# Banded attention and rational MLP in one kernel: scores and values in 64x32 tiles of TensorE, and a fixed issue order for the first three row tiles

## The chip, the cores and the metric

The kernel runs on one core of a Trainium2 chip. The time is device time in microseconds of one execution; three runs of the kernel before are given, and one further execution was recorded by the hardware profiler.

## The reference, cut to what matters

Eight batches of 576 positions, eight heads of 64 columns. Each query sees the 128 keys up to and including itself, with a bias that falls linearly with distance. The result, 4608 rows of 512 columns, goes through an MLP of width 2048 whose activation is a ratio of two polynomials.

```python
scores = scale * np.matmul(q, k.transpose(0, 1, 3, 2))
bias = slopes[:, None, None] * (-np.abs(rel).astype(np.float32))[None, :, :]
mask = (rel >= 0) & (rel < window)              # window = 128, rel = query - key
scores = np.where(mask, scores + bias[None], -1000000000.0)
attn = np.exp(scores - max); attn = attn / (sum + 1e-09)
x = np.matmul(attn, v)                           # heads side by side: 4608 x 512
h = x @ w_in; h2 = h * h; h3 = h2 * h            # 512 x 2048
P = a[0] + a[1] * h + a[2] * h2 + a[3] * h3
Q = 1.0 + np.abs(b[0]) * np.abs(h) + np.abs(b[1]) * h2
out = (P / (Q + 1e-06)) @ w_out                  # 2048 x 512
```

## The kernel before, in words

**Tiles.** The 4608 rows are 36 blocks of 128 rows, in 18 row tiles of two blocks. Heads go in pairs (four pairs `p`), one head of a pair on partitions 0 to 63 and the other on 64 to 127. The attention of one pair over one or two blocks is a **unit** (`attention(u)`, L411). Row tile 0 has eight units of one block, every other row tile four units of two blocks. Every ninth block (`kind == 1`, `own_only`) begins a batch and sees only its own keys.

**A unit.** TensorE makes the scores (`scores`, L441, matmuls at L456, result in PSUM tiles `sc0` and `sc1`, one per head). VectorE folds them into a dense 128x128 form: `copy_predicated` (L490) takes, where a mask says so, a score from a neighbouring column group, and L497 adds the bias and finds the row maximum. ScalarE takes the exponential (L502), VectorE the reciprocal of the sums (L510, L511), GpSimd scales the rows (`pr`, L512). TensorE transposes `pr` (L523); ScalarE copies the result into `p_all` (L529, L530, L532), GpSimd splits it into the part that belongs to the block's own keys and the part that belongs to the block before (L536). TensorE then multiplies with the values (`quarters`, L597, matmuls at L607, into PSUM tiles `px` and `py`; for row tile 0 and the last units of its kind `values`, L568, matmul L575), and ScalarE and VectorE bring the sum of both to SBUF as `x`, split into a coarse and a fine part (`x_hi`, `x_lo`).

**Tiles of TensorE.** Scores contract over the 64 columns of a head, so the array is used as 64 rows by 64 columns four times over (`tile_position=(64 * h, Q * half)`, `Q` = 64): the row half holds the head, the column half holds 64 of the 128 queries. The first 64 queries of a block need two calls (128 keys strided over the block before, then 64 own keys), the second 64 one call of 192 keys:

```python
elif half:
    todo = [(slice(0, 3 * Q), own - Q, own + P)]
else:
    todo = [(slice(0, 3 * Q, 2), own - P, own), (slice(Q, 2 * Q), own, own + Q)]
```

`quarters` uses the same four tiles: there the row half holds 64 keys and the column half one head's 64 value columns. From row tile 2 on, one plan entry issues the transposes of one unit, the scores of the next and the values of an earlier one back to back. This piece of TensorE's order is called a session here.

**MLP.** For each row tile and each of 16 chunks of 128 hidden columns, `up` (L730) makes `h` and `down` (L793) adds into `acc`; three fp32r matmuls for each product (`hi*hi`, `lo*hi`, `hi*lo`). In the first passes over row tiles 0 to 2 a chunk whose weights aren't split yet is used as plain fp32 (`is_plain`). The activation between them is L757 to L775 on ScalarE, GpSimd and VectorE.

**Weights.** They come as 64-bit numbers in 32 halves of 512 KB, one `raw_w` per chunk and matrix (loads L661 and L663), and `convert` turns each into fp32 with one step on GpSimd (L666), one on ScalarE (L667) and two on VectorE (L668, L669). `split` (L672) later makes the coarse and fine parts (L683, L684).

**Order.** Every step is an entry of `Plan` with costs per engine and a due time. `Plan.order` (L116) plays the entries through on modelled engines and queues, always the ready entry that is due first, and the order that comes out is the order in which the program issues them. All loads stand in SP's queue. The due times come from some sixty constants (L273 to L279).

## Time and profile before

| | us |
|---|---|
| three runs | 1016.33, 1017.22, 1017.29 (median 1017.22) |
| the profiled execution | 1016.81 |
| its span, first to last instruction | 1015.1 |
| TensorE (PE) busy | 997.9, 98% of the span |
| VectorE (DVE) busy | 789.5, 78% |
| ScalarE (ACT) busy | 693.0, 68% |
| GpSimd (POOL) busy | 513.7, 51% |

PE is the matmul stream, PEld the loading of stationary operands, which runs beside it. A plain fp32 matmul leaves two records in the trace, an fp32r one leaves one. A matmul's record holds its way through the array too, so records overlap, and the rate of a stream is read from the distance of the starts, not from the length of a record. `PEclk` is the granted share of TensorE's full clock.

### The profile page before, as it was taken

How to read it: one execution, taken by the hardware profiler on the slowest of the kernel's cores; microseconds unless marked ns; L12 is line 12 of the kernel's file. 1: busy time of each engine (PE TensorE's matmuls, PEld its weight loads, DVE VectorE, ACT ScalarE, POOL GpSimd, SP SyncE). 2: the span in 40 equal slices, each digit the busy share in tenths (PEclk: the TensorE clock that was granted, in tenths of full speed). 3: DMA queues.
4: the chain of work that ended last, by engine and by line, in shares of the span. 5: the costliest groups of instructions: out<-in, count | busy, mean ns of one | idle time of the engine just before them, and what ended most of it. 6: DMA issues, size and time to landing. Idle time of an engine off the chain costs nothing.

```text
span 1015.1 us, 24014 instructions
## 1 busy us (share of the span) xinstructions
PE 997.9 (98%) x9095; PEld 866.7 (85%) x9095; DVE 789.5 (78%) x1942; ACT 693.0 (68%) x1729; POOL 513.7 (51%) x567
## 2 busy tenths in 40 slices
PE   8899998999999999999999999999999999999998
PEld 4667777988888989998989999898898898998897
DVE  4889979788786878777787768787887786878775
ACT  5769777677766767676776666676766676767553
POOL 3757868454544544454555445544544544534432
PEclk7899999999999999999999999999999999999999
DMA  8845202111111111121211112021111211200000
GB/s 286 298 167 177 81 31 74 35 56 57 52 55 56 62 51 67 43 67 44 70 43 44 52 47 70 30 80 34 61 61 46 65 64 35 79 17 22 1 23 21
DMA packets 45139, 69.05 MB, mean 68 GB/s; under 512 B 4448, under 2 KB 29664, under 8 KB 45024
## 3 DMA queue, kind: packets, MB, share of 16 engines
q1 hardware_dynamic: 44736, 67.26, 20.5%
q8 instruction: 71, 1.16, 0.5%
q14 instruction: 44, 0.36, 0.1%
q10 hardware_dynamic: 288, 0.26, 0.1%
HBM read 58.07 MB, written 9.44 MB: 67 GB/s over the span
## 4 chain that ended last, share of the span: by engine, by line
PE 89%; POOL 3%; DMA 2%; DVE 2%; ACT 2%; issue 1%; SPq 0%; ACTq 0%; DVEq 0%; POOLq 0%
PE h L730 39%; PE acc L793 38%; PE sc L456 5%; PE px L607 4%; DMA raw_w<-in_w_in 1%; PE sc L523 1%; PE px L523 1%; POOL w_lo L684 1%; POOL g_q L760 1%; PE py L607 1%; POOL g_q L758 1%; DMA kq<-in_kqv 0%; POOL raw_w L666 0%; PE px L575 0%; DMA id_sb<-in_ident 0%
## 5 line engine op out<-in xcount | busy, mean ns | idle before, releaser
L730 PE MATMUL h<-x_hi,wi_hi 128*128 128x256 f32 x1024 | 289.2, 282 | 0.3 <-ACT x L612 0.2
L730 PE MATMUL h<-x_lo,wi_hi 128*128 128x256 f32 x1024 | 288.1, 281 | 0.2 <-DVE x_lo L618 0.2
L730 PE MATMUL h<-x_hi,w_lo 128*128 128x256 f32 x1024 | 287.5, 281 | 0.0
L758 POOL TENSOR_SCALAR g_q<-g_u,babs 128x512 f32<-128x512 f32 x144 | 112.1, 778 | 221.5 <-ACT g_u L757 210.9
L793 PE MATMUL acc<-wo_hi,g_h 128*128 128x512 f32 x532 | 215.3, 405 | 2.4 <-ACT g_h L774 2.4
L730 PEld LDWEIGHTS h<-x_lo,wi_hi 128*128 128x128 f32 x1024 | 192.8, 188 | 28.1 <-DVE x_lo L618 0.4
L793 PE MATMUL acc<-w_lo,g_h 128*128 128x512 f32 x532 | 209.1, 393 | 0.0
L730 PEld LDWEIGHTS h<-x_hi,wi_hi 128*128 128x128 f32 x1024 | 192.9, 188 | 18.2 <-ACT x L612 1.4
L793 PE MATMUL acc<-wo_hi,g_l 128*128 128x512 f32 x532 | 196.4, 399 | 0.0
L730 PEld LDWEIGHTS h<-x_hi,w_lo 128*128 128x128 f32 x1024 | 193.9, 189 | 0.0
L760 POOL TENSOR_TENSOR g_q<-g_q,g_u 128x512 f32<-128x512 f32 x144 | 186.6, 1296 | 10.8
L757 ACT ACTIVATE g_u<-h 128x512 f32<-128x512 f32 x144 | 86.0, 597 | 129.3 <-PE h L730 128.7
L761 DVE TENSOR_TENSOR g_p<-h,g_p 128x512 f32<-128x512 f32 x144 | 99.2, 689 | 89.8 <-ACT g_p L759 87.5
L512 POOL TENSOR_TENSOR pr<-pr,st 128x512 f32<-128x512 f32 (+1 forms) x76 | 76.1, 1002 | 179.6 <-DVE st L511 88.5
L766 DVE SCALAR_TENSOR_TENSOR g_q<-g_q,h 128x512 f32<-128x512 f32 x144 | 98.6, 684 | 60.4 <-ACT h L765 58.8
L763 ACT ACTIVATE g_u<-g_q,guard 128x512 f32<-128x512 f32 x144 | 104.7, 727 | 59.1 <-POOL g_q L760 58.8
L502 ACT ACTIVATE pr<-pr,st 128x128 f32<-128x128 f32 x288 | 113.5, 397 | 18.0 <-DVE st L497 17.3
L536 POOL TENSOR_SCALAR_AFFINE_SELECT p_all<-p_all 128x512 f32<-128x512 f32 (+1 forms) x144 | 91.1, 632 | 57.6 <-ACT p_all L530 49.0
L774 ACT CAST g_h<-h 128x512 fp32r<-128x512 f32 x133 | 78.0, 586 | 53.6 <-DVE h L773 43.2
L759 ACT ACTIVATE g_p<-h,na 128x512 f32<-128x512 f32 x144 | 112.2, 779 | 0.0
L793 PEld LDWEIGHTS acc<-wo_hi,g_h 128*128 128x128 f32 x532 | 100.0, 188 | 13.7 <-ACT g_h L774 3.8
L775 DVE TENSOR_TENSOR g_l<-h,g_h 128x512 fp32r<-128x512 f32 x133 | 91.1, 685 | 25.9 <-ACT g_h L774 25.3
(89 smaller groups left out, 1831.2 us busy)
## 6 DMA issues: line engine op xcount, KB each, us to landing
kq<-in_kqv SPq DMA_DIRECT2D x68, 320.0 KB, 3.5
v<-in_kqv SPq DMA_DIRECT2D x68, 192.0 KB, 2.7
out<-o SPq DMA_DIRECT2D x34, 256.0 KB, 2.1
raw_w<-in_w_in SPq DMA_DIRECT2D x16, 512.0 KB, 4.7
raw_w<-in_w_out SPq DMA_DIRECT2D x16, 512.0 KB, 4.8
bias_t<-in_bias SPq DMA_DIRECT2D x44, 64.0 KB, 2.5
kq<-in_kqv SPq DMA_DIRECT2D x4, 192.0 KB, 3.9
kq_first<-in_kqv SPq DMA_DIRECT2D x4, 128.0 KB, 2.8
```

The costliest lines, as they stand in the source:

```text
L502: nc.scalar.activation(ap(pr)[:, y, :], ap(pr)[:, y, :], AF.Exp, bias=ap(st)[:, y : y + 1], scale=-1.0, accum_out=ap(st)[:, 4 + y : 5 + y])
L536: plan.op(at + 0.6 - 0.1 * k, cost, lambda e, k=k, sign=sign: nc.gpsimd.affine_select(out=side(k), in_=side(0), pattern=[[0, 2], [0, m], [ ...
L730: nc.tensor.matmul(h(i), w[:, k, :], x[:, k, :], start=(k == 0 and m == 0), stop=(k == NKC - 1 and m == len(seq) - 1))
L757: plan.op(E, {"a": act(W, 1)}, lambda e: nc.scalar.activation(v(g_u), v(h_s), AF.Abs), reads=[(h_s, 0)], writes=[(g_u, 0)])
L758: plan.op(E, {"g": tsc}, lambda e: nc.gpsimd.tensor_scalar(v(g_q), v(g_u), ap(babs)[:, 1:2], ap(babs)[:, 0:1], ALU.mult, ALU.add), reads=[ ...
L759: plan.op(E, {"a": act(W, 1, 2) - 20}, lambda e: nc.scalar.activation(v(g_p), v(h_s), AF.Identity, bias=ap(na)[:, 2:3], scale=ap(na)[:, 3: ...
L760: plan.op(E, {"g": ttc}, lambda e: nc.gpsimd.tensor_tensor(v(g_q), v(g_q), v(g_u), ALU.mult), reads=[(g_q, 0), (g_u, 0)], writes=[(g_q, 0)])
L761: plan.op(E, {"v": dve(W)}, lambda e: nc.vector.tensor_tensor(v(g_p), v(h_s), v(g_p), ALU.mult), reads=[(h_s, 0), (g_p, 0)], writes=[(g_p, ...
L763: plan.op(E, {"a": act(W, 0, 1)}, lambda e: nc.scalar.activation(v(g_u), v(g_q), AF.Ln, bias=guard, scale=1.0), reads=[(g_q, 0)], writes=[ ...
L766: plan.op(E, {"v": dve(W)}, lambda e: stt(v(g_q), v(g_q), GUARD, v(h_s), ALU.add, ALU.mult), reads=[(g_q, 0), (h_s, 0)], writes=[(g_q, 0)])
L775: plan.op(E, {"v": dve(W)}, lambda e: nc.vector.tensor_tensor(v(g_l), v(h_s), v(g_h).bitcast(F32), ALU.subtract), reads=[(h_s, 0), (g_h, 0 ...
L793: nc.tensor.matmul(ap(accs[n][i]), x[:, sl], w, start=(c == c0 and part == 0 and m == 0), stop=(c == c1 - 1 and (part == 1 or plain) and m ...
```

## The change

**Scores.** The array is used as 64 rows by 32 columns, eight tiles. A column group of 32 queries needs 160 keys (its own 32 and the 128 before), in one call for the first and the last group of a block and in two calls (96 and 64) for the other two; `own_only` blocks take 128 keys in each group. A head's scores of one block are six calls where they were three, and lie in PSUM as six column groups of 32.

**Folding.** `copy_predicated` is issued once per head and half of the partitions, on half as many columns each, so four times per unit where it was two. The mask in `id_sb` is made by three small VectorE instructions at the start where it was one.

**Values.** `quarters` issues each of its products as two calls of 32 value columns each.

**Order.** `FIRST` lists 1,182 plan entries by number. `Plan.order` issues these as listed, each on its first engine or, where the number is negative, on its second, and goes on with due times after them. The planner's model of the DMA queue, one cost (1.5 for 1.4), the choice of the buffer that is reused, the cost of scores (330 for 388) and the constants of the due times have other values.

```diff
+FIRST = [
+    9, 10, 11, 12, 13, 14, 15, 24, 5, 38, 39, 0, 52, 66, 53, 25, 6, 160, 80, 26, 40, 27, 29, 28,
...
+        for code in FIRST:
+            o = self.ops[max(code, ~code)]
+            e = list(o.engines)[code < 0]
...
+            place(o, e, t)
...
-                closed = [(max(d.end + lat(d.engine, e) for d in x.left), n) for n, x in enumerate(ring) if x.open == 0]
-                ring.pop(min(closed)[1])
+                ring.remove(min((x for x in ring if x.open == 0), key=lambda x: max(y.rank for y in x.left)))
...
-        plan.op(-7, {"v": 100}, lambda e: nc.vector.memset(ap(id_sb)[:Q, 1, Q:], 0.0), reads=[(id_sb, 0)], writes=[(id_sb, 0)])
+        plan.op(-7, {"v": 130}, lambda e: nc.vector.tensor_scalar(ap(id_sb)[:Q, 1, :Q], ap(id_sb)[:Q, 1, :Q], -1.0, 1.0, ALU.mult, ALU.add), reads=[(id_sb, 0)], writes=[(id_sb, 0)])
+        plan.op(-7, {"v": 90}, lambda e: nc.vector.memset(ap(id_sb)[R:Q, 1, :R], 0.0), reads=[(id_sb, 0)], writes=[(id_sb, 0)])
+        plan.op(-7, {"v": 90}, lambda e: nc.vector.memset(ap(id_sb)[Q : 3 * R, 1, 3 * R :], 0.0), reads=[(id_sb, 0)], writes=[(id_sb, 0)])
...
+                own = (i + 1) * P
+                todo = []
+                for g in range(4):
+                    low, high = own - (4 - g) * R, own + (g + 1) * R
                     if own_only[i]:
-                        todo = [(slice(Q, 3 * Q), own, own + P)]
+                        calls = [(slice(R, 5 * R), own, own + P)]
                     else:
+                        calls = [
+                            [(slice(R, 6 * R), low, high)],
+                            [(slice(2 * R, 5 * R), low, own), (slice(R, 6 * R, 4), own, high)],
+                            [(slice(0, 5 * R, 4), low, own), (slice(R, 4 * R), own, high)],
+                            [(slice(0, 5 * R), low, high)],
+                        ][g]
+                    todo += [(n, g, *call) for n, call in enumerate(calls)]
+                for n, g, dst, k0, k1 in sorted(todo, key=lambda x: x[:2]):
+                    q = slice(R * g, R * g + R)
+                    for h in range(2):
...
+                        nc.tensor.matmul(to, qt(i)[r, q], kt(k0, k1)[r], start=True, stop=True, tile_position=(64 * h, R * g))
...
+                for half in range(2):
+                    q = slice(Q * half, Q * half + Q)
+                    spare = slice(0, R) if half else slice(5 * R, 6 * R)
+                    plan.op(A + 0.5, {"v": dve(Q * nb)}, lambda e, h=h, half=half, q=q, spare=spare: nc.vector.copy_predicated(
...
-                            d = slice(64 * h, 64 * h + 64)
-                            nc.tensor.matmul((ap(py) if half else px)[d, i, q0:q1], vt(i + own)[r, d], ap(w)[r, h, 2 * i + own, q0:q1], start=n == 0, stop=n == len(seen[0]) - 1, tile_position=(Q * half, 64 * h))
+                            for d0 in (64 * h, 64 * h + R):
+                                d = slice(d0, d0 + R)
+                                nc.tensor.matmul((ap(py) if half else px)[d, i, q0:q1], vt(i + own)[r, d], ap(w)[r, h, 2 * i + own, q0:q1], start=n == 0, stop=n == len(seen[0]) - 1, tile_position=(Q * half, d0))
```

**Where instructions move: TensorE, one session.** Before, the scores of an `own_only` block and of a full block and the first values of an earlier unit (the number behind a name is the buffer's):

```order
L456 MATMUL sc0_5939<-kq_5588 64x128
L456 MATMUL sc1_5941<-kq_5588 64x128
L456 MATMUL sc0_5939<-kq_5588 64x2x64
L456 MATMUL sc1_5941<-kq_5588 64x2x64
L456 MATMUL sc0_5939<-kq_5588 64x64
L456 MATMUL sc1_5941<-kq_5588 64x64
L456 MATMUL sc0_5939<-kq_5588 64x192
L456 MATMUL sc1_5941<-kq_5588 64x192
L607 MATMUL px_5943<-p_all_5753,v_5272 64x128 x2
L607 MATMUL py_5958<-p_all_5753,v_5272 64x128 x2
```

The full block is the last six score rows. In the changed kernel the same full block and the values behind it are

```order
L534 MATMUL sc0_6768<-kq_6016 32x160
L534 MATMUL sc1_6770<-kq_6016 32x160
L534 MATMUL sc0_6768<-kq_6016 32x96
L534 MATMUL sc1_6770<-kq_6016 32x96
L534 MATMUL sc0_6768<-kq_6016 32x2x32
L534 MATMUL sc1_6770<-kq_6016 32x2x32
L534 MATMUL sc0_6768<-kq_6016 32x160
L534 MATMUL sc1_6770<-kq_6016 32x160
L689 MATMUL px_6772<-p_all_6606,v_6007 32x128 x4
L689 MATMUL py_6799<-p_all_6606,v_6007 32x128 x4
```

where four more score rows (`32x2x32` and `32x96` for each head, the second calls of the two middle groups) stand between the last score row shown and the values. Twelve calls take the place of six, and sixteen value calls that of eight.

**GpSimd, the scaling of the ninth unit.** That unit is the first with two blocks; its `pr` is the one of 512 columns. The weight halves `raw_w` around it, before:

```order
L666 TENSOR_SCALAR raw_w6_269<-raw_w6_269 128x512
L536 AFFINE_SELECT p_all_380<-p_all_380 128x2x128 x2
L666 TENSOR_SCALAR raw_w3_279<-raw_w3_279 128x512
L512 TENSOR_TENSOR pr_382<-pr_382,st_383 128x256
L666 TENSOR_SCALAR raw_w8_336<-raw_w8_336 128x512
L666 TENSOR_SCALAR raw_w5_345<-raw_w5_345 128x512
L512 TENSOR_TENSOR pr_422<-pr_422,st_423 128x512
```

and in the changed kernel:

```order
L748 TENSOR_SCALAR raw_w1_299<-raw_w1_299 128x512
L593 TENSOR_TENSOR pr_421<-pr_421,st_422 128x256
L748 TENSOR_SCALAR raw_w6_328<-raw_w6_328 128x512
L748 TENSOR_SCALAR raw_w5_343<-raw_w5_343 128x512
L617 AFFINE_SELECT p_all_504<-p_all_504 128x2x128 x2
L593 TENSOR_TENSOR pr_478<-pr_478,st_479 128x512
L748 TENSOR_SCALAR raw_w8_375<-raw_w8_375 128x512
```

Eight weight halves stood ahead of this `pr` on GpSimd, the last of them the eighth load in SP's queue (`raw_w5_345`, with 7,811 KB of loads up to its end); now seven stand there, the last of them the seventh load (`raw_w5_343`, with 6,467 KB up to its end, as many as the sixth load `raw_w3_279` had before).

**SP, the first weight loads.** Before:

```order
L400 DMA v<-in_kqv 128x256
L319 DMA bias_std<-in_bias 128x1024
L400 DMA v<-in_kqv 128x256
L661 DMA raw_w_193<-in_w_in 128x4x256
L400 DMA v<-in_kqv 128x384
L661 DMA raw_w_212<-in_w_in 128x4x256
```

Now:

```order
L461 DMA v_first<-in_kqv 128x128 x2
L391 DMA ab_sb<-in_ab 128x6
L743 DMA raw_w_105<-in_w_in 128x4x256
L469 DMA kq<-in_kqv 128x384 x2
L461 DMA v_first<-in_kqv 128x128
L389 DMA bias_std<-in_bias 128x1024
L743 DMA raw_w_218<-in_w_in 128x4x256
```

The first weight half has moved ahead of the keys of row tile 0's second block, of the bias and of the first values of that block.

Of the 32 fine parts of the weights (L684, now L766) GpSimd makes 24 where it made 20, and VectorE 8 where it made 12.

## Rows read from the trace of the kernel before

**Rows 1.** The profile page, busy time of the engines: us, share of the span, instructions.

```profile
PE 997.9 (98%) x9095; PEld 866.7 (85%) x9095; DVE 789.5 (78%) x1942; ACT 693.0 (68%) x1729; POOL 513.7 (51%) x567
```

**Rows 2.** Busy time by stretch of the span: from:to, length, then busy us (and instructions) of PE, PEld, DVE, ACT and POOL, the granted clock, the share of the DMA engines and GB/s.

```profile
6.60:10.00 3.40, 1.76 (x19) 0.90 (x17) 0.87 (x8) 0.90 (x4) 1.18 (x2) 1.00 0.92 259
10.00:23.70 13.70, 11.80 (x97) 7.85 (x94) 8.74 (x39) 8.87 (x34) 7.04 (x13) 0.50 1.01 337
23.70:30.50 6.80, 2.91 (x44) 1.91 (x44) 5.28 (x24) 5.68 (x20) 4.76 (x9) 1.00 1.06 390
30.50:37.30 6.80, 6.36 (x26) 5.25 (x27) 6.54 (x11) 3.23 (x6) 4.63 (x9) 0.50 1.05 367
150.00:175.00 25.00, 22.30 (x230) 18.85 (x230) 23.57 (x54) 17.61 (x49) 22.10 (x21) 1.00 0.14 45
175.00:1000.00 825.00, 824.90 (x7806) 741.97 (x7805) 638.33 (x1557) 561.87 (x1401) 392.91 (x425) 1.00 0.16 50
1000.00:1015.10 15.10, 11.33 (x50) 8.92 (x48) 6.50 (x11) 4.41 (x8) 2.07 (x2) 0.95 0.10 35
```

**Rows 3.** Timeline of PE over one session in the middle of the span: start us, length us, line, result and operands, tile of the array, shape, number of records.

```profile
593.61 0.38 PE L523 MATMUL px<-id_sb,pr 128*128 128x128 f32 x2
593.92 0.94 PE L456 MATMUL sc<-kq 64*64 64x128 f32 x24
594.64 0.27 PE L607 MATMUL px<-p_all,v 64*64 64x128 f32 x1
...
594.86 0.22 PE L607 MATMUL px<-p_all,v 64*64 64x64 f32 x1
594.87 0.22 PE L607 MATMUL py<-p_all,v 64*64 64x64 f32 x1
594.91 0.22 PE L607 MATMUL px<-p_all,v 64*64 64x64 f32 x2
594.92 0.22 PE L607 MATMUL py<-p_all,v 64*64 64x64 f32 x2
594.97 0.22 PE L607 MATMUL px<-p_all,v 64*64 64x64 f32 x1
594.97 0.22 PE L607 MATMUL py<-p_all,v 64*64 64x64 f32 x1
594.98 0.27 PE L607 MATMUL px<-p_all,v 64*64 64x128 f32 x1
...
595.31 0.22 PE L607 MATMUL py<-p_all,v 64*64 64x64 f32 x1
595.46 0.50 PE L793 MATMUL acc<-wo_hi,g_h 128*128 128x512 f32 x1
```

**Rows 4.** Groups of instructions by line and shape: result and operands, tile, shape, number of records, busy us, mean ns of one.

```profile
L456 PE MATMUL sc<-kq 64*64 64x192 f32 x512 | 61.2, 353 | 0.0
L607 PE MATMUL px<-p_all,v 64*64 64x128 f32 x520 | 49.3, 270 | 0.0
L490 DVE COPY_PREDICATED sc<-id_sb,sc 128x256 f32<-128x256 uint32 x112 | 43.8, 421 | 4.2 <-ACT p_all L529 4.0 <-PE sc L456 0.2
L490 DVE COPY_PREDICATED sc<-id_sb,sc 128x128 f32<-128x128 uint32 x32 | 8.1, 289 | 3.5 <-PE sc L456 3.3
L511 DVE RECIPROCAL st<-st 128x4 f32<-128x4 f32 x68 | 11.8, 174 | 1.4
L684 DVE TENSOR_TENSOR w_lo<-w,wo_hi 128x512 fp32r<-128x512 f32 x7 | 6.9, 992 | 2.1 <-PE acc L793 1.7 <-ACT wo_hi L683 0.4
L684 DVE TENSOR_TENSOR w_lo<-w,wi_hi 128x512 fp32r<-128x512 f32 x5 | 5.1, 1021 | 0.6 <-POOL w_lo L684 0.6
L318 DVE MEMSET id_sb<- 64x64 f32 x1 | 0.1, 112 | 1.2 <-DMA id_sb<-in_ident 1.2
```

**Rows 5.** Timelines of POOL, DVE and PE between 24 and 34 us, in brackets the idle time before an instruction and what ended it.

```profile
25.20 0.92 POOL L536 TENSOR_SCALAR_AFFINE_SELECT p_all<-p_all 128x256 f32<-128x256 f32 x2
26.10 0.67 POOL L666 TENSOR_SCALAR raw_w<-raw_w 128x512 f32<-128x512 f32 x1
27.95 0.66 POOL L666 TENSOR_SCALAR raw_w<-raw_w 128x512 f32<-128x512 f32 x1 [0.61 <-DMA raw_w<-in_w_in]
29.25 0.64 POOL L666 TENSOR_SCALAR raw_w<-raw_w 128x512 f32<-128x512 f32 x1 [0.64 <-DMA raw_w<-in_w_out]
29.85 1.04 POOL L512 TENSOR_TENSOR pr<-pr,st 128x512 f32<-128x512 f32 x1
28.92 0.18 DVE L511 RECIPROCAL st<-st 128x4 f32<-128x4 f32 x1
30.95 1.12 PE L523 MATMUL pt<-id_sb,pr 128*128 128x128 f32 x4 [3.12 <-POOL pr L512]
33.04 2.08 PE L736 MATMUL h<-x_plain,w 128*128 128x128 f32 x8
```

**Rows 6.** Who PE waited for between 100 and 200 us: us in total, times, longest.

```profile
PE acc L793 <- ACT g_h L774: 2.4, 4, 0.9
```

More of the change, by code (lines that the diff above doesn't have):

```diff
@@ L39 @@
 MASKED = -8.0e9
+FIRST = [
[50 rows of a table added]
+]
 GUARD = 1.0 + 1e-6
@@ L77 @@
 class Op:
-    __slots__ = ("due", "engines", "emit", "deps", "slots", "left", "users", "start", "end", "engine", "after", "follows", "rows", "sb")
+    __slots__ = ("rank", "due", "engines", "emit", "deps", "slots", "left", "users", "start", "end", "engine", "after", "follows", "rows", "sb")
 class Plan:
@@ L141, in order @@
         self.index = {o: i for i, o in enumerate(self.ops)}
-        for o in self.ops:
-            if o.left == 0:
-                push(o)
-        events = [0.0, 650.0]
-        seen = {0.0}
+        events, seen = [], set()
         def wake(x):
@@ new lines, in order @@
+        for code in FIRST:
+            o = self.ops[max(code, ~code)]
+            e = list(o.engines)[code < 0]
+            t = max([free_at[e]] + [d.end + lat(d.engine, e) for d in o.deps])
+            for s in o.slots:
+                ring = rings.get(s.tag, [])
+                if s.turn is None and len(ring) == s.bufs:
+                    old = min((x for x in ring if x.open == 0), key=lambda x: max(y.rank for y in x.left))
+                    t = max([t] + [d.end + lat(d.engine, e) for d in old.left])
+            place(o, e, t)
@@ L191, in order @@
+        for o in self.ops:
+            if o.engine is None and o.left == 0:
+                push(o)
+        for x in list(free_at.values()) + [r[0] for e in ready for r in ready[e]]:
+            wake(x)
         while n < total:
@@ L212, in order @@
                     o = best[3]
[L213 to L240 removed]
+                    place(o, e, t)
                     ready[e].remove(best)
[L242 to L243 removed]
                     wake(free_at[e])
@@ L462, in attention @@
         bank = slot(ps3, [P, 4 * P], F32, "px", tag="h") if turned or held else None
-        cost = SESSION + sum(215 if x else 388 for x in own_only)
+        cost = SESSION + sum(215 if x else 330 for x in own_only)
         emits, reads, writes = [scores], list(kq_keys), [(sc[0], 0), (sc[1], 0)]
```

116 lines of the change are left out of this document (56 added, 60 removed), and 49 rows, old and new, of the table FIRST.

## The prediction

> **What bounds the kernel now.** I read the page's busy times first: PE 98% of a span of 1015.1 us, VectorE 78%, ScalarE 68%, GpSimd 51% [rows 1]. Then the same by stretch: from 175 to 1000 us PE is busy 824.90 of 825.00 us, the others well below [rows 2]. In this long part, four fifths of the span, only a shorter stream of matmuls makes the kernel shorter, and every nanosecond taken from it counts in full as long as no other engine becomes late; VectorE, the next, has 638.33 of 825. The start is another matter: PE idles 17.2 us of the span, about 3.8 in the last 15.1 us (the last rows leaving) and nearly all the rest before 175 us, 2.7 of it between 150 and 175 [rows 1, 2]. Twice in the start its granted clock stands at 0.50, that is 1.2 of 2.4 GHz: from 10.0 to 23.7 us, after a stretch in which it was busy 1.76 of 3.40 us, and from 30.5 to 37.3, after 2.91 of 6.80 [rows 2].
>
> **What a session costs.** The timeline of one session [rows 3] gives the price of work in 64x64 tiles. Values: the first record of the first block starts at 594.64, that of the second block at 594.98. In these 0.34 us each of the four tiles takes 128 and 64 columns twice (two records per matmul), so the four tiles run at the same time and 192 columns cost 0.34 us. Scores: two blocks from 593.92 to 594.64, 0.72 us. Each tile again has 192 columns per block, 2 x 0.34 = 0.68, and 0.04 is left for filling the tiles at the start of the session. What follows the scores starts without a gap, and the switches from and to the whole array (593.61 to 593.92, 595.31 to 595.46) stay in number and place.
>
> **Part 1, scores in eight tiles.** If eight tiles run as four do, a block costs 160 columns per tile where it cost 192: 0.34 x 160/192 = 0.283, which saves 0.057 us. There are 512 records of 64x192 [rows 4], two per matmul and two heads per block, hence 128 full blocks: 128 x 0.057 = 7.3 us. Blocks with 128 columns per tile keep them. Against it stands the filling: twice as many calls have to go out before all tiles work. That is nothing more at best, and twice 0.04 us at worst in each of 68 sessions of two blocks (68 reciprocals of four columns [rows 4]), 2.7 us. Bounds 7.3 and 4.6; nothing in the rows is nearer to one, so I take the middle, **5.9 us less**. Nearly all sessions lie in the PE-bound part, so the term reaches the end.
>
> **Part 2, values in the same tiles.** A tile has the same 128 and 64 columns, in eight tiles of half the width: no gain in columns, and no switch of form between scores and values, which there was none of before. Twice the calls cost nothing if tiles start independently, which is the rival below. Taken as 0.
>
> **Part 3, folding on VectorE.** One instruction of 128 partitions x 256 columns takes 421 ns, one of 128 columns 289 ns [rows 4]. On half the partitions and half the columns I take the time by columns: two of 289 for one of 421, and for one-block units, by the same slope of 132 ns per 128 columns, two of 223 for one of 289: +157 ns each time, 144 times, 22.6 us on VectorE. From 175 to 1000 that makes some 655 of 825 us, 79%, still far from PE's share, and the chain of a unit grows by 0.31 us, which the sessions ahead of it cover. If that cover were gone, it would be PE waiting for GpSimd's `pr`. In the start the attention chain is on the path, since PE waits there: I count one unit's lengthening, **0.3 us more**. The mask's two extra small instructions are of the kind that takes 112 ns [rows 4], while VectorE waits for loads anyway: 0.
>
> **Part 4, the fixed list.** It costs the chip nothing by itself; it moves instructions. What I can follow:
> - PE's longest wait is 3.12 us before the transposes at 30.95, for GpSimd's `pr`, which started at 29.85 behind two weight halves that waited 0.61 and 0.64 us for their loads [rows 5]. Now the seventh load stands last ahead of it, with as many KB up to its end as the sixth had, and the sixth was worked on at 26.10 with no wait. So GpSimd could begin `pr` at 26.10 + 0.67 + 0.92 = 27.7 [rows 5]. But `pr` also needs VectorE's reciprocal, which ended at 28.92 + 0.18 = 29.1, and that one is late next: its chain is not shorter. 29.85 less 29.1 leaves 0.75 at best, 0 at worst; I take **0.6 less**, near the best since the loads alone allow more. From 33.04 PE has the MLP, so it carries.
> - PE waits 2.4 us four times for ScalarE's `g_h` between 150 and 175 us [rows 6], while VectorE, which makes its input, is busy 23.57 of 25.00 us [rows 2]. Four of VectorE's 12 fine weight parts, about 1 us each [rows 4], go to GpSimd; two or three sessions there add 0.8 at 0.31 each. GpSimd is busy 22.10 of 25.00 us itself. All 2.7 may go, or 0.8 may come; I take half of the gap, **1.3 less**.
> - The clock: PE is busy 6.36 us of the stretch at 1.2 GHz from 30.5 to 37.3. At 2.4 GHz that would be 3.2 less. Since PE's long wait ahead of it hardly shrinks, I count 0, and keep 3.2 as a bound.
> - Worst: the list makes one more such hole, 3.1 us of waiting and 3.2 of work at half the clock after it, 6.3 us.
>
> **Sum.** -5.9 + 0.3 - 0.6 - 1.3 = -7.5 us, against the profiled execution's 1016.81: 1009.3. The median of the three runs is 0.4 above that execution, so I predict **1009.7 us**, 0.7% less. A measurement of this kernel tells about 0.2%, 2 us, from no change.
>
> **Rivals.**
>
> *A. Small records have a floor in each row half (slower).* The smallest records shown, 64 columns, come four to a row half (`px`) between 594.86 and 594.98, 0.03 us each [rows 3]. That is what two tiles at once give by columns, but it could also be the rate at which a row half takes records. Then scores, with 12 records per block and row half, cost 12 x 0.03 = 0.36, as now (0.72 / 2), and values with 16 records 0.48 where they cost 0.34: +0.14 on 130 blocks (520 records of 64x128 for `px`, four per block [rows 4]), +18.2. With -1.6 from parts 3 and 4: 1016.8 + 16.6 + 0.4 = 1033.8 us. It decides from about 0.0245 us per record up, where 16 records cost 0.392 in values (+6.8 us over all) and scores save 0.046 x 128 = 5.9; from 0.021 down values lose nothing. Against it: two `px` records start within the same hundredth at 594.91, and 594.97 is followed by 594.98, so no fixed distance is kept [rows 3]. Chance 0.10.
>
> The Trainium skill (TensorE: Matmul & The Clock Gate, "Wait — 56ns, not 53.3ns?") has a rule that speaks against this change: the distance from start to start never falls below about 25 ns, however few columns. As one floor for the whole engine it disagrees with this trace, where the 32 records of values start from 594.64 to 595.31, 21 ns each. Taken for each row half, an estimate by its 0.025 us is 0.40 for a block's values (+7.8 us) and 0.30 for its scores (-5.1), and with -1.6 a time of 1018.3, no change.
>
> *B. The list loses in the start what sessions win.* The hole of 6.3 us above, in place of parts 3 and 4, and -5.9: 1017.6 us. For it: the start hangs on loads that keep the DMA engines busy (1.05 to 1.06 [rows 2]), and weights that come earlier make keys and values come later. Against it: on PE and GpSimd the order of the first units has changed by a few places only. Chance 0.12.
>
> *C. Four column tiles of a row half don't run together,* so that the change of form isn't one in time. If a row half feeds two at a time, scores cost 0.34 x 2 x 160/192 = 0.57 and values 0.68: +0.21 x 128 + 0.34 x 130 = +71, 1087 us. Nothing in this trace has four column tiles; two do run together [rows 3]. Chance 0.03. The Trainium skill (same page, "Measured speedup vs the span model") reports sixteen tiles at 10.6 times; by that C doesn't arise, and no run here shows it.
>
> *D. Both parts at their best:* -7.3, -0.75, -2.7 and -3.2: 1003.3 us. Chance 0.10.
>
> **How the numbers follow.** The forecast itself has 0.65; its own bounds, 4.6 to 7.3 for part 1 and the ends of the two waits, make 1007 to 1014. The range of 8 in 10 reaches down past D and up past B and the milder floor of A, to take in a hole somewhat longer than the one priced: **1002 to 1019 us**. Outside are most of A, C and the tails of B and D, nearly 2 in 10. Faster: forecast, D and a small part of B, 0.77. Within 0.2%: part of B and of A, 0.07. Slower: most of A, C and part of B, 0.16.
>
> **What would show it.** Scores in a session of two full blocks should take 0.57 to 0.65 us from their first record to the first value record, values 0.34 per block as before; values at 0.40 or more mean A, and 0.6 and more C. VectorE's folding should read near 290 ns, 288 times. PE should be as fully busy from 175 us on as now; if it is not, the longer chain of part 3 is the first suspect. In the start, compare PE's wait before the ninth unit's transposes, the stretch at half clock, and the idle time between 150 and 175 us. A loss there of more than 6 us would make the prediction wrong in spite of right sessions.

## The result, and the profile after

The changed kernel takes **1025.32 us** (median of 4 runs, 1024.31 to 1025.86); the kernel before took 1016.83 on the same chip. The ratio is 1.0083, 95% interval [1.0071, 1.0095]: **0.8% slower**, where 0.7% faster was forecast. The profiled execution took 1025.05 us with a span of 1023.3.

The page's busy line, to be set against [rows 1]:

```profile
PE 1005.3 (98%) x12743; PEld 873.0 (85%) x12743; DVE 838.4 (82%) x2084; ACT 698.2 (68%) x1729; POOL 519.9 (51%) x571
```

TensorE has 3648 more matmul records and is 7.4 us longer busy; VectorE has 48.9 us more. The same stretches as [rows 2], columns as there:

```profile
6.60:10.00 3.40, 2.52 (x46) 1.19 (x44) 1.75 (x14) 2.00 (x8) 1.19 (x3) 1.00 0.84 243
10.00:23.70 13.70, 9.87 (x180) 6.72 (x178) 10.82 (x47) 8.74 (x32) 7.68 (x15) 0.75 1.06 374
23.70:30.50 6.80, 3.74 (x43) 2.73 (x32) 6.35 (x25) 6.28 (x21) 5.70 (x10) 0.75 1.03 377
30.50:37.30 6.80, 6.21 (x130) 5.27 (x129) 6.49 (x11) 3.34 (x7) 3.67 (x6) 0.75 0.67 238
150.00:175.00 25.00, 23.80 (x360) 21.44 (x341) 23.61 (x57) 20.13 (x51) 20.62 (x18) 1.00 0.23 76
175.00:1000.00 825.00, 823.82 (x10778) 738.90 (x10778) 670.22 (x1659) 560.48 (x1393) 395.26 (x425) 1.00 0.15 49
```

The start got better: more work before 10 us, about 14 us at the lower clock where there were 20 (the length of each stretch times 2 x (1 - granted clock), added up), and 1.2 us of idle time between 150 and 175 where there were 2.7. From 175 us on PE is nearly as fully busy as before, so what was lost there was lost in the length of its own work. A session of two full blocks, as in [rows 3] (rows left out are marked with dots):

```profile
589.51 0.38 PE L604 MATMUL px<-id_sb,pr 128*128 128x128 f32 x2
589.83 0.84 PE L534 MATMUL sc<-kq 64*32 64x160 f32 x41
590.43 0.29 PE L689 MATMUL px<-p_all,v 64*32 64x128 f32 x1
590.44 0.34 PE L534 MATMUL sc<-kq 64*32 64x64 f32 x4
...
590.50 0.30 PE L534 MATMUL sc<-kq 64*32 64x96 f32 x3
...
590.90 0.22 PE L689 MATMUL px<-p_all,v 64*32 64x64 f32 x1
590.91 0.25 PE L689 MATMUL py<-p_all,v 64*32 64x64 f32 x4
590.96 0.32 PE L689 MATMUL px<-p_all,v 64*32 64x128 f32 x3
...
591.31 0.29 PE L689 MATMUL py<-p_all,v 64*32 64x64 f32 x6
591.53 0.39 PE L812 MATMUL h<-x_hi,wi_hi 128*128 128x256 f32 x1
```

The first value starts sooner, 0.60 us after the first score, where 0.72 were read before. The scores themselves don't end sooner: 41 of their 48 records stand ahead of that first value and seven behind it (590.44 and 590.50), while in [rows 3] all 24 stand ahead. In the new form a value record starts while other tiles still have scores. The values take longer: from the first block's first record to the second's 0.53 us (before 0.34; some of it are those seven score records), and on to the next whole-array matmul 0.57 (before 0.48). The groups that answer to [rows 4], columns as there:

```profile
L534 PE MATMUL sc<-kq 64*32 64x160 f32 x1024 | 63.6, 309 | 0.7 <-DVE w L751 0.6
L689 PE MATMUL px<-p_all,v 64*32 64x128 f32 x1040 | 61.5, 276 | 0.0
L571 DVE COPY_PREDICATED sc<-id_sb,sc 64x128 f32<-64x128 uint32 x224 | 60.4, 293 | 7.7 <-ACT p_all L610 3.5 <-PE sc L534 0.9
L571 DVE COPY_PREDICATED sc<-id_sb,sc 64x64 f32<-64x64 uint32 x64 | 13.4, 228 | 6.8 <-ACT p_all L610 4.2 <-PE sc L534 1.6
```

A values record of 128 columns lasts 276 ns, as before (270): the single record did not get slower, the records got more. The folding is what was forecast, 293 and 228 ns.

Over the 44 sessions of two full blocks that start after 100 us the medians are, worked out from the records' start times (score part: first score to first value; value part: from there to the next whole-array matmul; last score: start of the last score record, counted from the first; the last columns count the calls in a session):

| kernel | score part | value part | session, us | last score | score calls | value calls |
|---|---|---|---|---|---|---|
| before | 0.718 | 0.818 | 1.536 | 0.667 | 12 | 16 |
| after | 0.608 | 1.099 | 1.708 | 0.708 | 24 | 32 |

After the change the two parts overlap: the value part holds the last 0.100 us of scores. All 62 sessions after 100 us together take 93.05 us before and 103.39 after, **10.3 us more**; the medians of the runs differ by 8.5. The list made up for a part in the start; the experiments say how much, and what else was lost there.

### The profile page after: what moved, and what is told of

It is laid out like the page before. It is cut to its first block, busy times and chain, and to the rows that moved or that the text cites. A ratio compares the mean times of both kernels' runs of the same rounds, so it can differ in the third digit from the quotient of the medians.

```text
span 1023.3 us, 31565 instructions
## 1 busy us (share of the span) xinstructions
PE 1005.3 (98%) x12743; PEld 873.0 (85%) x12743; DVE 838.4 (82%) x2084; ACT 698.2 (68%) x1729; POOL 519.9 (51%) x571
## 4 chain that ended last, share of the span: by engine, by line
PE 82%; DVE 9%; ACT 3%; POOL 2%; issue 2%; DMA 1%; SPq 1%; ACTq 0%; DVEq 0%; POOLq 0%
PE h L812 34%; PE acc L875 34%; PE sc L534 5%; PE px L689 2%; PE py L689 2%; PE px L604 1%; DVE h L849 1%; PE sc L604 1%; DVE sc L571 1%; DVE g_q L848 1%; DVE pr L578 1%; POOL g_q L842 1%; DVE x_lo L700 1%; DVE g_p L843 1%; DVE g_l L857 1%
## 5 line engine op out<-in xcount | busy, mean ns | idle before, releaser
L875 PE MATMUL acc<-wo_hi,g_l 128*128 128x512 f32 x532 | 201.4, 399 | 0.0
L849 DVE SCALAR_TENSOR_TENSOR h<-g_p,na,h 128x512 f32<-128x512 f32 x144 | 108.2, 752 | 1.2
L844 DVE SCALAR_TENSOR_TENSOR g_p<-g_p,na,h 128x512 f32<-128x512 f32 x144 | 107.1, 744 | 2.4
```

What stands on the lines that cost most here:

```text
L844: plan.op(E, {"v": dve(W, 1)}, lambda e: stt(v(g_p), v(g_p), ap(na)[:, 1:2], v(h_s), ALU.add, ALU.mult), reads=[(h_s, 0), (g_p, 0)], write ...
L849: plan.op(E, {"v": dve(W, 1)}, lambda e: stt(v(h_s), v(g_p), ap(na)[:, 0:1], v(h_s), ALU.add, ALU.mult), reads=[(g_p, 0), (h_s, 0)], write ...
L875: nc.tensor.matmul(ap(accs[n][i]), x[:, sl], w, start=(c == c0 and part == 0 and m == 0), stop=(c == c1 - 1 and (part == 1 or plain) and m ...
```

## The experiments

Twelve kernels ran, each beside the kernel before on its chip. Three theories of the value part stood at first: **Q**, that a session goes by its number of calls, which reach the array through one queue; **H**, rival A, that each row half takes a record every 0.03 us; **S**, rival C, that the column tiles of a row half share its columns. "Against before" is the difference of the medians on the same chip.

| run | edit | median, us | against before | ratio, 95% interval | score / value part, us |
|---|---|---|---|---|---|
| change | | 1025.32 | +8.5 | 1.0083 [1.0071, 1.0095] | 0.608 / 1.099 |
| e1 | change, values in 64x64 | 1026.04 | +9.4 | 1.0093 [1.0078, 1.0108] | 0.908 / 0.828 |
| e2 | change, px and py in turn | 1024.14 | +7.5 | 1.0072 [1.0057, 1.0087] | 0.608 / 1.083 |
| e3 | change, 16 of 64 columns | 1021.48 | +4.9 | 1.0049 [1.0034, 1.0064] | 0.608 / 1.035 |
| e4 | change, all tiles 64x64 | 1007.73 | -8.9 | 0.9912 [0.9896, 0.9929] | 0.718 / 0.818 |
| e5 | e4, four long folds | 1028.10 | +11.4 | 1.0115 [1.0098, 1.0132] | 0.718 / 0.818 |
| e6 | e4, values in 64x32 | 1026.45 | +9.7 | 1.0095 [1.0080, 1.0110] | 0.868 / 0.979 |
| e7 | change, 8 py calls fewer | 1017.92 | +1.2 | 1.0012 [1.0002, 1.0021] | 0.608 / 0.943 |
| e8 | e4, 300 list entries | 1029.48 | +12.7 | 1.0120 [1.0105, 1.0135] | 0.718 / 0.817 |
| e9 | e4, four folds of the change's size | 1015.78 | -1.2 | 0.9989 [0.9980, 0.9999] | 0.718 / 0.818 |
| e10 | change, two folds of four | 1018.60 | +1.7 | 1.0017 [1.0008, 1.0027] | 0.607 / 1.098 |
| e11 | change, 8 score calls fewer | 1015.17 | -1.8 | 0.9983 [0.9974, 0.9992] | 0.567 / 0.955 |
| e12 | e4, 900 list entries | 1013.08 | -3.9 | 0.9965 [0.9952, 0.9978] | 0.718 / 0.817 |

**e1, values back in 64x64 tiles.**

```diff
-for d0 in (64 * h, 64 * h + R):
-    d = slice(d0, d0 + R)
-    nc.tensor.matmul(..., tile_position=(Q * half, d0))
+d = slice(64 * h, 64 * h + 64)
+nc.tensor.matmul(..., tile_position=(Q * half, 64 * h))
```

> The changed kernel with its values back in four 64x64 tiles (8 calls a block for 16), scores still in eight. All theories: values return to 0.34 us a block, scores stay at 0.61 us a session, and what is new is a switch of form between them, bounded by the switches that the trace shows, 0.15 to 0.31 us. Session 1.43 + 0.15 to 0.31 = 1.58 to 1.74 us for 1.71 now, so 0.13 less to 0.03 more on 62 sessions: 1017 to 1027 us. If the values aren't what costs, the session stays at 1.71 or above.

The value part falls back to 0.828, but the time does not fall. A session of this kernel (timeline of PE):

```profile
591.49 0.98 PE L534 MATMUL sc<-kq 64*32 64x160 f32 x48
592.40 0.33 PE L688 MATMUL px<-p_all,v 64*64 64x128 f32 x2
592.41 0.33 PE L688 MATMUL py<-p_all,v 64*64 64x128 f32 x2
...
593.07 0.22 PE L688 MATMUL py<-p_all,v 64*64 64x64 f32 x2
593.23 0.38 PE L811 MATMUL h<-x_hi,wi_hi 128*128 128x256 f32 x1
```

The first value record starts 0.91 us after the first score instead of 0.60. Not all of these 0.30 us are the switch of form: all 48 score records now stand ahead of it, the last at 0.707 us as in the change. From there to the first value it is 0.201 us, where the kernel before, without a switch, has 0.051 (0.718 less 0.667). The switch costs the difference, 0.15 us. With the scores no shorter than before, eight tiles for the scores alone gain nothing here.

**e2, the value calls of the two row halves in turn.**

```diff
-for half in range(2):
-    for h in range(2):
-        for d0 in (64 * h, 64 * h + R):
+for d0 in range(0, P, R):
+    for half in range(2):
```

> The changed kernel with the same 64x32 value calls issued with the two row halves (px, py) in turn, where four px calls and then four py calls stood. Theory Q (calls reach the array in program order through a queue of limited length and rate, so four calls of one half keep the other half waiting): values fall from 1.10 us a session towards 0.82, kernel 1008 to 1020. Theory H (each row half takes a record every 0.03 us, whatever the order) and theory S (the four column tiles of a row half share what they are fed): order changes nothing, 1025.

The value part is 0.017 us shorter. The order in which the halves are fed hardly matters.

**e3, the second product of the values on 16 columns instead of 64.**

```diff
 own, q0, q1 = seen[half][n]
+q1 = q0 + 16 if n else q1
```

> The changed kernel with the second value call of each product on 16 columns where it has 64 (the other 48 columns of that part of the result are left without it): 144 columns a tile and block for 192, the same number of calls. Theories Q and H (cost by number of calls): values stay at 1.05 to 1.10 us a session, 1022 to 1025 us. Theory S (cost by columns): values fall by a quarter of 0.95, to 0.86, and the kernel by 15 us, to 1010.

Three quarters of the columns of half of the value calls are gone, and the value part falls by 0.064 us, where S wanted some 0.24. S falls: the price is not mainly one of columns.

**e7, eight calls fewer in one row half.**

```diff
-for half in range(2):
+for half in range(1 if n else 2):
```

> The changed kernel without the second product of the lower row half of the values (the four calls of 64 columns into py per block): 24 value calls per full session instead of 32, all eight gone from one row half, while the other row half keeps its 16 calls (32 records). It leaves out a part of the values, so its result is not the reference's. Theory H (a row half takes a record each 0.03 us): the other half still sets the time, values 1.07 to 1.10 us, 1024 to 1025.5 us. Theory Q (all calls share one rate, about 33 ns per call once the stock is used up): values 0.82 to 0.88 us, 62 sessions by 0.22 to 0.28 us less, 1008 to 1012 us. In between (0.95 us) neither holds alone.

The half of `px` keeps all of its records, and yet the value part falls by 0.156 us. H, a limit of each row half by itself, falls too. Q's number was missed the other way: 0.943, where 0.82 to 0.88 was expected, 0.0195 us per call left out.

**e11, eight score calls fewer with the same columns.**

```diff
-[(slice(2 * R, 5 * R), low, own), (slice(R, 6 * R, 4), own, high)],
-[(slice(0, 5 * R, 4), low, own), (slice(R, 4 * R), own, high)],
+[(slice(R, 6 * R), low, high)],
+[(slice(0, 5 * R), low, high)],
```

> The changed kernel with one call of 160 columns for each score tile, where the two middle tiles of a block take two calls (96 and 64 columns): 16 score calls per full session instead of 24, the same columns in all. The keys of the middle tiles then stand in other places, so the result is not the reference's. Theory Q (calls come one each 16.7 ns once the stock of 17 is used up, so a session's length goes by its calls): the score part ends with the stock, 0.48 to 0.52 us instead of 0.61, values unchanged at 1.08 to 1.12, a session 1.57 to 1.60 instead of 1.71, and 1016 to 1018.5 us. Rival (columns set the length): sessions 1.69 to 1.72 us, 1024 to 1026 us. A price per call of more than one place in the queue would give below 1.55 us.

The number of columns, the form and the values' own calls are as in the change, and the session is 0.186 us shorter, more than Q asked for. Its session in the timeline of PE:

```profile
597.20 0.77 PE L534 MATMUL sc<-kq 64*32 64x160 f32 x32
597.76 0.27 PE L689 MATMUL px<-p_all,v 64*32 64x128 f32 x1
...
598.52 0.27 PE L689 MATMUL py<-p_all,v 64*32 64x64 f32 x5
598.72 0.39 PE L812 MATMUL h<-x_hi,wi_hi 128*128 128x256 f32 x1
```

All 32 score records stand ahead of the first value here. The last one starts 0.478 us after the first, where the change has 0.708: the scores themselves give back 0.230 us, 29 ns for each call left out. From the last score on, the session takes 1.044 us, 0.044 more than in the change, whose values had begun among the last scores. So the fall of the value part, by 0.144 us, doesn't say that the values got faster. The first value comes after 0.567 us, twice the 0.283 that the prediction gave to 160 columns: with one call for each column group the scores do run as forecast. (The run changes the number of calls and the way the columns are split at once.) The expected 16.7 ns per call was too low (0.186 / 8 = 23 ns came), and the score part lies above the 0.48 to 0.52 us of Q.

**e6, the values alone in eight tiles**, on top of e4.

```diff
-d = slice(64 * h, 64 * h + 64)
-nc.tensor.matmul(..., tile_position=(Q * half, 64 * h))
+for d0 in (64 * h, 64 * h + R):
+    d = slice(d0, d0 + R)
+    nc.tensor.matmul(..., tile_position=(Q * half, d0))
```

> The kernel of e4 with the values alone in eight tiles of 64x32 (32 calls of 32 columns wide weights per session instead of 16); scores and folding as before the change. No part of the result changes. Theory Q (calls reach the array in program order from a stock that fills while earlier work runs, and out of the stock they come no faster than about 33 ns each): the 12 score calls run for 0.72 us, long enough for the stock to fill, so the value part takes less than in the changed kernel, 0.82 to 0.95 us instead of 1.10, and the time is 1009 to 1015 us if the change of form inside a session costs nothing. Theory H (a row half takes a record each 0.03 us, whatever came before): values 1.07 to 1.12 us, 1022 to 1027 us. If the change of form costs as in e1 (0.3 us between the scores and the first value), it shows in the first part of the session (0.72 to 1.0 us) and adds up to 18 us in either theory.

Neither theory's number: the value part is 0.979 us, between Q's 0.82 to 0.95 and H's 1.07 to 1.12, and the switch of form costs 0.150 us here (0.868 against 0.718), as much as in e1. With 12 score calls ahead of them, 32 value calls take 0.161 us more than 16 do (0.979 against 0.818). They take 0.955 us behind 16 score calls (e11). So what the values take hardly depends on the calls ahead of them, and Q's stock that fills meanwhile is not shown.

**The sessions by their last score record.** The same sessions as in the table above, start times in us from the first score record:

| kernel | tiles of scores, values | calls | last score | first value | last value | whole-array matmul |
|---|---|---|---|---|---|---|
| before, e4 | 64x64, 64x64 | 12 + 16 | 0.667 | 0.718 | 1.388 | 1.536 |
| e6 | 64x64, 64x32 | 12 + 32 | 0.667 | 0.868 | 1.702 | 1.848 |
| e1 | 64x32, 64x64 | 24 + 16 | 0.707 | 0.908 | 1.588 | 1.737 |
| change | 64x32, 64x32 | 24 + 32 | 0.708 | 0.608 | 1.562 | 1.708 |
| e7 | 64x32, 64x32 | 24 + 24 | 0.707 | 0.608 | 1.405 | 1.551 |
| e11 | 64x32, 64x32 | 16 + 32 | 0.478 | 0.567 | 1.377 | 1.522 |

The first four add up to within 0.02 us: scores in eight tiles cost 0.04 us, values in eight tiles 0.13 to 0.16, a switch of form 0.15 in either direction.

**e4, all tiles back to 64x64, the list and the constants kept.** Scores, folding (two copies of 128 partitions) and values are those of the kernel before; the list's entries for the other two folds and the other mask steps emit nothing.

```diff
-plan.op(A + 0.5, {"v": dve(Q * nb)}, lambda e, ...: nc.vector.copy_predicated(
-    out=parts4(sv(h)[q, bs, R + Q * half : R + Q * half + Q]), ...
+plan.op(A + 0.5, {"v": dve(Q * nb)}, lambda e, ...: None if half else nc.vector.copy_predicated(
+    out=parts3(sv(h)[:, bs])[:, :, 1:], ...
```

> The changed kernel's plan and fixed list with scores, folding and values all in the form of before (64x64 tiles, two copy_predicated a unit). What the list and the new constants do alone. Sessions 1.54 us for 1.71, 62 of them: 10.4 less than 1025.3, so 1015 if the start keeps its gain; 1017 if the list gains nothing; over 1019 if the list costs.

1007.73 us, the best kernel of this study, 0.9% below the kernel before. The tile forms with all that hangs on them cost 17.4 us, and the list with its constants is worth 8.9. Where it gains shows first in its busy line on the page:

```profile
PE 989.3 (98%) x9095; PEld 864.0 (86%) x9095; DVE 803.4 (80%) x1938; ACT 696.6 (69%) x1729; POOL 520.1 (52%) x571
```

and in three of its windows (columns as in [rows 2]):

```profile
6.60:10.00 3.40, 2.50 (x29) 1.24 (x28) 1.49 (x11) 1.97 (x9) 1.23 (x3) 1.00 0.88 238
10.00:23.70 13.70, 9.85 (x121) 7.27 (x121) 10.92 (x46) 9.42 (x35) 8.60 (x16) 0.88 1.05 371
23.70:30.50 6.80, 4.59 (x32) 3.75 (x29) 6.37 (x21) 6.29 (x18) 5.59 (x9) 0.75 1.07 399
```

PE executes the same 9095 records in 8.6 us less busy time than in [rows 1], and its idle time is 1.3 us less. From 10 to 23.7 us, where the granted clock was 0.50 [rows 2], it is 0.88. By granted clock and length about 20 us stood at 1.2 GHz before, about 7 here, in two stretches:

```profile
16.39:19.80 3.41, 3.41 (x28) 3.02 (x28) 2.94 (x12) 2.88 (x9) 2.62 (x5) 0.50 1.05 398
26.63:30.04 3.41, 3.28 (x19) 2.96 (x20) 3.31 (x6) 3.06 (x7) 3.01 (x5) 0.50 1.07 396
```

PE is busy 6.7 us in them; before, it was 18.2 (11.80 and 6.36 [rows 2]).

**e8 and e12, the list cut.**

```diff
-for code in FIRST:
+for code in FIRST[:300]:      # e12: FIRST[:900]
```

> The kernel of e4 with only the first 300 entries of the list of 1142 or so; from there the planner orders the work by its due times and the new constants. No part of the result changes. It tells where the 9 us that e4 gains over the kernel before come from. Theory L1 (the gain lies in the first entries: first weights loaded earlier, no stretch at half clock): 1007 to 1010 us. Theory L2 (the order of units later in the start matters as much): 1011 to 1016 us. If the list does nothing and the new constants alone do it, L1's number comes out too, and the lead over the kernel before at the first units of work (-4.7 us in e4) tells: by the list it stays at -4 to -5, since the 300 entries cover that.

> The kernel of e4 with the first 900 of the 1182 entries of the list (e8 had 300 and lost 22 us against e4, between 20 and 100 us into the run). No part of the result changes. If the list's worth lies in keeping the order of the first units together through the stretch that e8 lost, 900 entries bring it back: 1006 to 1011 us. If the list is worth something only when it reaches to the point where the planner's own order is steady, it loses again at the place where it ends: 1013 to 1025 us, with the loss after 100 us.

With 300 of the 1182 entries the gain of 8.9 us becomes a loss of 12.7; with 900, 3.9 are kept. L1 falls, L2 stands and is larger than expected. e8's two longest waits of PE between 50 and 100 us (total, times, longest) show a part of it, 6.7 us in a stretch in which e4 has no idle time of PE; its granted clock there is 0.90, where e4 has 1.00.

```profile
PE sc L594 <- DVE w L740: 4.4, 1, 4.4
PE acc L864 <- DVE g L841: 2.3, 1, 2.3
```

e12 was expected at 1006 to 1011 or at 1013 and more with the loss after 100 us; the second came, barely. At equal work of the MLP it is 0.7 us behind e4 at 143 us and 7.7 at 218. These two tell of the list with the new constants, not of the old order: the planner with the constants alone was not timed.

**e5 and e9, the folding's price with the tiles left alone.**

```diff
 # e5: each fold of e4 as two copies of 64 partitions
+for half in range(2):
+    q = slice(Q * half, Q * half + Q)
-    out=parts3(sv(h)[:, bs])[:, :, 1:], ...
+    out=parts3(sv(h)[q, bs])[:, :, 1:], ...
 # e9: and each of them on half its columns
+    out=parts3(sv(h)[q, bs])[:, :, 1:, :R], ...
```

> The kernel of e4 (scores and values back in 64x64 tiles, the list and the new constants kept; 1007.7 us), with one edit: each folding of a unit is done by two copies of 64 partitions instead of one of 128, so four per unit as in the changed kernel. No part of the result changes. It takes the VectorE cost of Part 3 (22.6 us more on VectorE) by itself; TensorE's sessions keep the old form (0.72 / 0.82 us). e4 is about 17.6 us below the changed kernel, of which about 10.5 us lie in the sessions and 7 us do not. Theory F (the 7 us outside the sessions are the longer folding, mostly in the start, where VectorE's results are waited for): 1012.5 to 1015, and the loss against e4 has come up by 240 us into the run. Rival (the folding is covered everywhere, as the prediction put it, and the 7 us come from longer attention sessions in the start): 1007.5 to 1009.

> The kernel of e5 with each of the four copies of a unit's folding cut to half its columns, so that the folding has the shape and length that the change gives it (64 partitions, 128 elements for two blocks, about 0.29 us, four per unit) while scores and values stay in 64x64 tiles. It leaves out the folding of the other half of the score columns, so its result is not the reference's. e5's copies were 0.397 us each, twice the elements of the change's, and put 61 us on VectorE over e4 and 20 us on the time: an overdose, of which a third came through. Here VectorE should be about 22 to 30 us above e4's 803.4. Theory F (Part 3 was no covered cost: what VectorE gets in the first 250 us comes through to about a third): 1014 to 1017 us, lost against e4 by 250 us into the run. Rival (e5 lost because its copies crossed a limit that the change's do not reach): 1008 to 1010 us.

e5 missed its numbers (1012.5 to 1015) far on the upper side, because it is not the change's dose: its copies take as long as the whole ones, so VectorE had 61 us more than in e4, not 22.6. e9 has the right size. The group of its copies:

```profile
L562 DVE COPY_PREDICATED sc<-id_sb,sc 64x128 f32<-64x128 uint32 x224 | 60.4, 293 | 7.2 <-ACT p_all L601 3.5 <-PE sc L526 0.5
```

Its windows from 50 to 250 us, and under them those of e4:

```profile
50.00:100.00 50.00, 47.87 (x301) 33.18 (x292) 47.07 (x116) 39.11 (x92) 34.90 (x42) 1.00 0.47 154
100.00:250.00 150.00, 146.95 (x1346) 123.53 (x1345) 133.65 (x324) 111.46 (x278) 101.17 (x102) 1.00 0.20 64
```

```profile
50.00:100.00 50.00, 50.00 (x292) 33.97 (x290) 45.72 (x102) 38.78 (x90) 35.90 (x42) 1.00 0.42 137
100.00:250.00 150.00, 148.76 (x1411) 127.10 (x1410) 129.82 (x311) 114.31 (x287) 100.18 (x102) 1.00 0.22 68
```

The copies are the change's (293 ns, 224 times), VectorE has 31.4 us more than in e4, the time is 1015.78 us: **7.7 us lost** against e4 (each set against its own runs of before) by four short copies instead of two long ones, with sessions as long as before. VectorE is at 94% between 50 and 100 us, and PE, never idle there in e4, idles 2.1 us, in one wait for VectorE; 1.8 more in the next 150. At equal work of the MLP the two are 2.5 us apart at 39 us, 6.4 at 250 and 7.9 at the end. Theory F holds: the copies are not covered in the start. The wait (total, times, longest):

```profile
PE h L802 <- DVE g L842: 2.1, 1, 2.1
```

**e10, the reverse: two of the change's four copies left out.**

```diff
-lambda e, h=h, half=half, q=q, spare=spare: nc.vector.copy_predicated(
+lambda e, h=h, half=half, q=q, spare=spare: None if half else nc.vector.copy_predicated(
```

> The changed kernel with two of its four folding copies per unit left out (those of the lower 64 partitions); it leaves out that part of the scores, so its result is not the reference's. The reverse of e9: VectorE falls by some 40 us, to e4's level, and the sessions keep the new form (0.61 / 1.10 us). Theory F: the part of the loss that is not in the sessions goes away, 1016 to 1019 us. Rival (the loss outside the sessions comes from their length in the start, not from VectorE): 1024 to 1025.5 us.

1018.60 us, within what F expected: 6.8 us come back, with sessions of 1.706 us. The same two windows of this kernel:

```profile
50.00:100.00 50.00, 49.90 (x394) 34.16 (x395) 45.38 (x107) 39.52 (x93) 35.81 (x42) 1.00 0.44 146
100.00:250.00 150.00, 149.00 (x2019) 126.53 (x2018) 125.98 (x302) 112.19 (x282) 100.61 (x101) 1.00 0.21 65
```

With less on VectorE PE is again all but fully busy (0.1 and 1.0 us idle).

**The sum from the runs.** By e4, e9 and the change: the list -8.9, the folding +7.7, the eight tiles +9.7, together +8.5. By e4, e10 and the change, in the other order: -8.9, tiles +10.6, folding +6.8. (e10 has some 13 us less on VectorE than e4, so its split favours neither.) The sessions by themselves, 103.39 us against e4's 92.19, are 11.2.

## Why the prediction was wrong

Forecast and measurement are 16.0 us apart (-7.5 and +8.5). By the runs, scores account for 9.1 of them, values for 7.1 and folding for 6.5 to 7.4, and the list took 7.0 off, together 15.7 to 16.6.

**Part 1 is the step that missed most:** "If eight tiles run as four do, a block costs 160 columns per tile where it cost 192". That was to win 5.9 us. By their last score record the scores of the 62 sessions take 42.9 us where they took 39.7, **3.2 us lost**. The sign that was named for it, 0.57 to 0.65 us from the first score to the first value, came out at 0.608 by luck: the prediction took the first value for the end of the scores, and in eight tiles it isn't. The price by columns was right where each column group has one call (e11, 0.567 us for the two blocks, twice the forecast 0.283). It left out that two of the four groups need a second call.

**Part 2 failed too:** "Twice the calls cost nothing if tiles start independently ... Taken as 0." From the last score record to the whole-array matmul the 62 sessions take 60.5 us where they took 53.4, **7.1 us lost**; per block, values cost 0.07 to 0.08 us more (change and e6). Both steps looked for the limit inside the array, in columns and tiles, and asked whether tiles start independently, not how fast calls follow one another. Tiles do start independently, as the values among the last scores show. But a session's 28 calls became 56. In 64x32 tiles 56 calls start within 1.562 us and 48 within 1.377 (e11) or 1.405 (e7), 28 to 29 ns per call; before, 28 calls took 1.388 us, 50 ns each, which the price by columns explains. Leaving out eight of 56 gives back 0.156 us (e7) or 0.186 (e11), among the values or among the scores, and leaving out columns gives little (e3).

Rival A comes near: it wanted the scores of a session at 0.72 us as before (0.708 by the last record) and the values 0.14 more per block (0.07 to 0.08). The sign that was named for it, 0.40 us or more per block, was met with 0.53, but that holds the late score records too. And its mechanism, a floor in each row half, wanted e7 unchanged, and e7's sessions are 0.157 us shorter with all records of one row half kept.

The rule weighed in the prediction, of the Trainium skill (TensorE: Matmul & The Clock Gate, "Wait — 56ns, not 53.3ns?"), that starts never stand closer than about 25 ns, disagrees with this trace as a floor: the session's 112 records start within 1.562 us, 14 ns each. Its direction, that small matmuls cost by their number, was right. Taken for each row half it gave 0.30 us for a block's scores, where 0.35 came by the last record, and 0.06 more than before for its values, where 0.07 to 0.08 came; and e7 shows that the row half is not what limits. The time by it, 1018.3 us, lay closer than the forecast.

**Part 3 was right in VectorE's time and wrong in its cover.** 293 and 228 ns were measured for the forecast's 289 and 223, which makes 23.8 us more of folding for 22.6. The cover named, "the sessions ahead of it", holds for most of what follows 250 us, where e9 lost 1.5 of its 7.9 us. In the start VectorE is itself near its limit, 94% in some stretches, and not one unit's lengthening but the added work of all early units reaches the end: +6.8 to +7.7 us in all for a term of 0.3. A row had hinted at it: VectorE busy 23.57 of 25 us between 150 and 175 [rows 2].

**Part 4 was right in sign and mis-sized:** -8.9 for -1.9, the list with its constants. Both its named gains came. The ninth unit's `pr` (timelines of POOL, DVE and PE, as [rows 5]):

```profile
26.15 1.26 POOL L748 TENSOR_SCALAR raw_w<-raw_w 128x512 f32<-128x512 f32 x2
28.42 1.04 POOL L593 TENSOR_TENSOR pr<-pr,st 128x512 f32<-128x512 f32 x1
28.13 0.18 DVE L592 RECIPROCAL st<-st 128x4 f32<-128x4 f32 x1
29.55 1.11 PE L604 MATMUL pt<-id_sb,pr 128*128 128x128 f32 x4
30.46 1.91 PE L818 MATMUL h<-x_plain,w 128*128 128x128 f32 x8
```

`pr` now starts right behind the reciprocal, which is itself 0.8 us earlier, and PE does not wait for it; the MLP's matmuls follow at 30.46 instead of 33.04, 2.6 us for the 0.6 counted. The gap of PE between 150 and 175 us shrank by 1.5 for the 1.3 counted, with its wait for `g_h` between 100 and 200 us (compare [rows 6]):

```profile
PE acc L875 <- ACT g_h L856: 1.7, 2, 0.9
```

What was missed is in the main the clock. Only the second stretch at 1.2 GHz was priced, as a bound of 3.2; the first, 11.80 busy us from 10.0 to 23.7 [rows 2], was not, and it is the larger. In e4 most of it is gone; PE is busy 2.50 of the 3.40 us ahead of it instead of 1.76. The 18.2 busy us at 1.2 GHz became 6.7. Half of the difference, 5.7 us, is an estimate of what the clock gave, of 8.6 us less busy time; the rest is not accounted for. How the clock and the folding act on each other in the start is open: the change and e10 have about 14 us at the lower clock, e4 and e9 about 7.

**Rivals.** B, the hole in the start, is half right: no hole came from the list, but VectorE's work took some 6 us there. C did not arise. D's assumption on the scores did not come true in the change; e11 has it.

**What stays open.** Why calls of 64x32 tiles don't follow faster than one in 28 ns. Each call brings the loading of its own stationary operand with it (as many PEld as PE records on the page), and no run separates the two. In the change's sessions the loads of the first 17 calls come close together, then none starts for 0.136 us, and then they come 16.7 ns apart for a while; e11, too, has 16.7 ns from its eighteenth call on. That fits calls arriving at a limited rate, as Q has it, but a run that varies nothing but that rate was not made. How e11's gain divides between fewer calls and columns split otherwise is open too.

## What to carry to other kernels

Cutting matmuls into smaller tiles trades columns for calls: count the calls of the whole back-to-back piece, and price them beside the columns. Where tiles run independently, read the end of a part from its own last record; the first record of the next part can stand well ahead of it. A test that leaves out calls at equal columns tells calls from columns in one run. And "VectorE is at 80%" says nothing of the start: look for cover in the stretch in which the added work runs, and price every stretch at the lower clock, not only the one beside the wait that is moved.

## What the runs showed of the hardware

- A switch between 64x32 and 64x64 tiles inside a session costs 0.15 us in either direction: from the last score record to the first value 0.201 us in e1 and in e6, 0.051 in the kernel before, which has no such switch.
- In sessions of 64x32 tiles calls follow one another at 28 to 29 ns on average, over 56 calls (the change) and over 48 (e7, e11).
- A `copy_predicated` on 64 partitions with 256 columns takes 427 ns (e5's row below), on 128 partitions 421 [rows 4]: half the partitions save nothing.

```profile
L562 DVE COPY_PREDICATED sc<-id_sb,sc 64x256 f32<-64x256 uint32 x224 | 90.2, 427 | 6.8 <-ACT p_all L601 3.5 <-PE sc L526 0.2
```

- An order of work fixed for the first row tiles, with the planner's new constants, was worth 8.9 us with the tiles unchanged. The same 9095 records of PE took 8.6 us less busy time, with about 7 instead of 20 us at the lower clock.
